# A new order of work and fixed engines in an attention plus two-layer kernel

## The chip, the cores and the metric

One core of one Trainium2 chip. The metric is device microseconds of one execution of the program on that core, the median of several runs. The profiled execution is one more run, taken with the hardware profiler.

## What is computed

Attention with a position bias, then two feed-forward networks, each on 2304 tokens of width 512 with an inner width of 2048:

```python
# _attn_ref: q, k, v are (4, 8, 576, 64)
scores = scale * np.matmul(q, k.transpose(0, 1, 3, 2))
...
x = (psi_rel / psi_i)[..., None]
h = np.maximum(x @ w1 + b1, 0.0)
bias = h @ w2
scores = scores + bias.transpose(2, 0, 1)[None, :, :, :]
scores = scores - np.max(scores, axis=-1, keepdims=True)
attn = np.exp(scores)
attn = attn / (np.sum(attn, axis=-1, keepdims=True) + 1e-09)
return np.matmul(attn, v).astype(np.float32)
...
# _moe_ref
h = x @ w_in
r = np.maximum(h, 0.0)
g = s * (r * r) + b
return (g @ w_out).astype(np.float32)
...
# _moe2_ref
h = x @ w_in
g = h - np.tanh(h)
return (g @ w_out).astype(np.float32)
```

## The kernel before

Matrix products run in f16 on pairs: every operand is split into a high part (a cast) and a low part (what the cast lost), and three products are summed. The splits run on VectorE (`DVE`), ScalarE (`ACT`) and GpSimd (`POOL`); DMAs are issued by SyncE (`SP`).

**Attention** runs over units, each one head of one batch and 128 (or twice 64) query rows: 144 units in groups of four. One unit takes these steps, named by the function inside `unit_tasks` and `unit_rest`: a bias load (`fn`, tile `bi`, DMA), scores (`qk`, two units at a time, L981), bias added and row minimum (`ttr`, L1013 and L1017, VectorE; called the max below, since the sign is turned), exponential (`ex`, L1023, ScalarE), high part (`hi`, L1033 on VectorE or L1035 on ScalarE), low part (`lo`, L1042, GpSimd, two instructions), a DMA transpose of both parts (`tr`, tile `et`, L1048), and the product with the values (`pv`, L1061 and L1067). Every four units `x_tasks` scales the output, splits it and transposes it by DMA into `xt`. The bias itself is made ahead, in 36 strips (`bias_tasks`): hidden values (L667, L670), a matmul (L701), two scaled copies (L558 or L560, tile `et`), a store.

**First feed-forward** (`moe1_tasks`) runs over nine blocks of 256 tokens beside the attention: matmuls into `ph` (L1477), relu and square, high and low part (L1500, L1504), matmuls into `po` (L1546), evacuation `out`, store to `x2d`. Its weights arrive as f64, are turned to f32 on VectorE (L1172 to L1178), and split.

**Second feed-forward** starts when attention has given its memory free (`turn`): its weights are loaded and converted too, then 18 steps `k` (half a block each) run `in_product` (tag `I`, L1942) and `out_product` (tag `J`, L2070), seven products of 24 matmuls each per step, with the products of step k-1 written between those of step k. Between the two lie small sums, tanh and splits; each step has seven high casts (L558 on VectorE or L560 on ScalarE, the two-engine lambda in `split`) and seven low parts (L563, VectorE). `prep_tasks` (tag `X`) prepares a block.

**The order of work** is planned when the program is built. Each step is a `Task` with, for every engine that may run it, a cost in us (for a DMA a pair: how long SyncE is held, how long the transfers are busy). `Schedule.forward` replays the machine with these costs: it takes the engine that can start first, and among its ready tasks the one with the least `prio`; the order found is the order in which the instructions are written to each engine. An engine takes its instructions in that order. `prio` is a due time from the code plus a number from `SHIFT` for that task's key (tag and function name). `COST` multiplies a cost by kind and engine. `HOP` is the time until another engine sees a result, `OVER` what is taken off until the engine is free, `LATE` what its own next step waits. A DMA lands `DMA_START` + its transfer time + `DMA_DONE` after its issue if nothing queues. `ONLY` fixes an engine for a kind. A load's base cost stands in the calls of `load`; a transpose's (1.25, 1.4) in `unit_rest`.

Of the kernel before, what the change touches and what calls it, by code (L numbers as in the profile page):

```python
# [30 lines left out]
AHEAD = 6.0  # L31
COST = {
    "u.ex@act": 1.056, "u.hi@act": 1.132, "bias.lambda@act": 1.102, "f.relu@act": 0.952, "f.square@act": 1.145,
    "x.lambda@act": 1.198, "w.lambda@act": 1.131, "scan.sq@act": 1.17, "bias.out@act": 1.146, "f.out@act": 1.282,
    "w.square@act": 1.07, "k.hi@act": 1.147, "s.lambda@act": 1.093, "q.hi@act": 1.201, "v.hi@act": 1.142,
    "u.ttr@dve": 1.025, "f.hi@dve": 1.09, "x.scale@dve": 0.9, "x.hi@dve": 1.03, "u.hi@dve": 1.07, "s.in_done@dve": 1.78,
    "scan.add@dve": 0.73, "f.lambda@dve": 0.96, "s.out_done@dve": 1.2, "u.lo@pool": 0.947, "f.lo@pool": 0.918,
    "bias.lambda@pool": 0.95, "u.qk@pe": 0.885, "u.pv@pe": 0.97,
}
PORT = {"u.ttr": 0.0, "x.scale": 0.0, "scan.add": 0.0, "k.lambda": 0.4, "v.lambda": 0.4, "q.lambda": 0.4, "s.lambda": 0.4,  # L40
    "X.scales": 0.0, "X.sums": 0.0, "f.scales": 0.0, "f.out": 0.0, "f.norm": 0.0, "w.scales": 0.0, "L.scales": 0.0, "scan.lambda": 0.0,
}
ONLY = {"I.fn": "dve", "I.sub": "dve", "J.fn": "dve", "J.c22": "dve", "I.add": "dve", "X.xsum": "dve", "P.wsum": "dve", "u.lo": "pool", "f.lo": "pool"}
EPS, WINDOW, IDLE, BUSY = 0.02, 3.4, 0.6, 0.9
SHIFT = {
# [162 lines left out]
class Schedule:  # L208
# [11 lines left out]
    def add(self, opts, fn, deps=(), prio=0.0, takes=(), uses=(), after=(), share=None):  # L220

        t = Task()
# [2008 lines left out]
```

## Time and profile before

| what | value |
|---|---|
| median of 3 runs | 1087.64 us (1086.15 to 1091.06) |
| profiled execution | 1087.81 us |
| its span, first to last instruction | 1086.0 us |
| mean granted clock of TensorE | 0.945 |
| TensorE matmul busy | 974.0 us, 90% |
| VectorE busy | 888.1 us, 82% |
| ScalarE busy | 685.5 us, 63% |
| GpSimd busy | 345.7 us, 32% |

Engines: PE is the matmul and PEld the weight load of TensorE, DVE VectorE, ACT ScalarE, POOL GpSimd, SP SyncE. A share over the whole span mixes stages with different limits; the rows below are cut by stage. A wait is put down to what ended it last.

### The profile page before, as it was taken

Reading aid. Unit: us, or ns where it says so; the run is one execution under the profiler, and the core shown is the slowest. Engines: PE = TensorE matmul, PEld = TensorE weight load, DVE = VectorE, ACT = ScalarE, POOL = GpSimd, SP = SyncE. Lnnn points to the kernel's source line nnn. Section 1 sums busy time; section 2 is a strip of 40 time slices with the busy share of each in tenths; the row PEclk is TensorE's granted clock in tenths of the full one; section 3 lists DMA queues with packets and bytes.
Section 4 is the critical chain, followed back from the end, with each engine's and each line's share of the span. In section 5 each row is a group of like instructions: output and inputs, shape, how many; then the busy total and the mean of one; then the engine's idle time right before and its main releaser. Section 6 shows DMA issues by size and latency. Waiting matters only on the chain.

```text
span 1086.0 us, 32355 instructions
## 1 busy us (share of the span) xinstructions
PE 974.0 (90%) x13370; PEld 823.4 (76%) x13370; DVE 888.1 (82%) x1881; ACT 685.5 (63%) x1313; POOL 345.7 (32%) x370
## 2 busy tenths in 40 slices
PE   5566788999999899989889898997999999999998
PEld 2222356678877677777678687887999999999998
DVE  6999999758579766876662989898999999998785
ACT  6698888779765666765663475556665546455452
POOL 5024557446473465665752323210000000000000
PEclk9756599999999999999999899998999999999999
DMA  9979987999989999999985903410010110100000
GB/s 340 355 223 232 284 214 143 215 211 264 247 163 202 189 179 188 205 166 175 161 165 115 353 16 114 159 35 6 27 46 32 31 31 22 41 22 22 21 22 21
DMA packets 261443, 153.65 MB, mean 141 GB/s; under 512 B 197680, under 2 KB 229552, under 8 KB 261296
## 3 DMA queue, kind: packets, MB, share of 16 engines
q1 hardware_dynamic: 261296, 151.59, 57.6%
q8 instruction: 104, 1.70, 0.7%
q14 instruction: 43, 0.35, 0.1%
HBM read 84.03 MB, written 20.33 MB: 96 GB/s over the span
## 4 chain that ended last, share of the span: by engine, by line
PE 52%; DVE 16%; DMA 14%; ACT 7%; issue 5%; POOL 4%; SPq 2%; DVEq 0%; ACTq 0%; POOLq 0%
PE acc L2070 13%; PE po L1546 10%; DMA et<-hl 10%; PE pa L1942 9%; PE pb L1942 6%; PE ph L1477 6%; POOL hl L1042 2%; DVE sp L1013 2%; PE po L2070 2%; PE sp L981 2%; POOL hr L1504 2%; PE xp L1061 2%; DVE w1big L1175 1%; ACT e L1023 1%; DVE hr L1500 1%
## 5 line engine op out<-in xcount | busy, mean ns | idle before, releaser
L1042 POOL TENSOR_TENSOR hl<-e,hl 128x64 f16<-128x64 f32 (+1 forms) x288 | 232.7, 831 | 233.1 <-ACT hl L1035 114.1
L1546 PE MATMUL po<-hr,w1big 128*128 128x256 f16 x1728 | 208.5, 277 | 12.4 <-POOL hr L1504 4.8
L1546 PEld LDWEIGHTS <-w1big 128*128 128x128 f16 x1728 | 167.7, 100 | 40.4 <-issue 18.9
L1477 PEld LDWEIGHTS <-w1big 128*128 128x128 f16 x1728 | 166.6, 99 | 25.8 <-issue 6.1
L1942 PEld LDWEIGHTS <-w2big 128*128 128x128 f16 x3024 | 175.7, 99 | 2.4 <-issue 2.3
L2070 PEld LDWEIGHTS <-w1big 128*128 128x128 f16 x3024 | 174.2, 98 | 4.1 <-issue 4.1
L1013 DVE CUSTOM_DVE_ANT_0 sp<-sp,bi 128x576 f32<-128x576 f32 x144 | 109.6, 761 | 45.4 <-PE sp L981 34.0
L1023 ACT ACTIVATE e<-sp,mx 128x576 f32<-128x576 f32 x144 | 105.8, 736 | 58.2 <-DVE mx L1017 48.8
L1504 POOL TENSOR_TENSOR hr<-r,hr 128x512 f16<-128x512 f32 x72 | 99.1, 1378 | 126.1 <-DVE hr L1500 118.0
L1477 PE MATMUL ph<-xt_own,w1big 128*128 128x256 f16 x960 | 111.4, 273 | 0.9 <-ACT r L1490 0.9
L1061 PEld LDWEIGHTS <-et 128*128 128x128 f16 (+1 forms) x1440 | 52.3, 103 | 70.5 <-DMA et<-hl 54.1
L1061 PE MATMUL xp<-vp,et 128*128 128x64 f16 (+1 forms) x1440 | 65.4, 198 | 37.5 <-DMA et<-hl 35.6
L981 PE MATMUL sp<-ks,qs 64*128 64x288 f16 (+1 forms) x960 | 82.0, 302 | 9.9 <-ACT e L1023 7.7
L1477 PE MATMUL ph<-w1big 128*128 128x256 f16 x768 | 90.5, 278 | 0.0
L2070 PE MATMUL acc<-hr,w1big 128*128 128x128 f16 x1296 | 81.5, 221 | 4.0 <-DVE hr L563 4.0
L1035 ACT ACTIVATE hl<-e 128x576 f16<-128x576 f32 x95 | 64.7, 682 | 24.6 <-DMA et<-hl 23.3
L2070 PE MATMUL acc<-w2big,w1big 128*128 128x128 f16 x1296 | 79.0, 219 | 0.0
L1500 DVE CAST hr<-r 128x512 f16<-128x512 f32 x72 | 46.3, 644 | 30.7 <-ACT r L1495 28.0
L981 PEld LDWEIGHTS <-qs 64*128 64x128 f16 (+1 forms) x960 | 45.7, 101 | 33.8 <-issue 21.1
L1490 ACT ACTIVATE r<-ph 128x512 f32<-128x512 f32 x72 | 42.5, 592 | 37.6 <-PE ph L1477 30.0
L1942 PE MATMUL pa<-w1big,w2big 128*128 128x128 f16 x960 | 62.8, 224 | 2.2 <-ACT w1big L1961 2.2
L1495 ACT ACTIVATE r<-r,sq 128x512 f32<-128x512 f32 x72 | 51.7, 720 | 1.1
(222 smaller groups left out, 1696.3 us busy)
## 6 DMA issues: line engine op xcount, KB each, us to landing
bi<-btd SPq DMA_DIRECT2D x64, 288.0 KB, 3.8
w1big<-in_wout SPq DMA_DIRECT2D x12, 1024.0 KB, 6.2
btd<-et SPq DMA_DIRECT2D x36, 295.5 KB, 3.2
w1big<-in_win SPq DMA_DIRECT2D x8, 1024.0 KB, 8.0
w2big<-in_win SPq DMA_DIRECT2D x8, 1024.0 KB, 12.6
x2d<-x SPq DMA_DIRECT2D x36, 128.0 KB, 2.3
w1big<-x2d SPq DMA_DIRECT2D x36, 128.0 KB, 2.5
outT<-xt_own SPq DMA_DIRECT2D x18, 256.0 KB, 2.2
```

Source lines behind the costliest of these rows:

```text
L981: nc.tensor.matmul(out=out, lhsT=qs.tile[64 * h:64 * h + 64, sq, p * r:p * r + r], rhs=ks.tile[64 * h:64 * h + 64, sk, half * HS:(half + 1 ...
L1013: nc.vector.tensor_tensor_reduce(out=st, in0=st, in1=bi.tile.rearrange("p (a b) -> p a b", a=2), scale=-1.0 / KAP, scalar=3.0e38, op0=ALU. ...
L1023: nc.scalar.activation(out=put(e, row_tile("e")).rearrange("p (a b) -> p a b", a=2), in_=sp.tile[:, :, 0:HS], func=AF.Exp, scale=-1.0, bia ...
L1035: nc.scalar.activation(out=h[:, 0:S], in_=e.tile, func=AF.Copy)
L1042: (nc.gpsimd if eng == POOL else nc.vector).tensor_tensor(out=hl.tile[:, o:o + m], in0=e.tile[:, c:c + m], in1=hl.tile[:, c:c + m], op=ALU ...
L1061: nc.tensor.matmul(out=xp[r0:r0 + r, o:o + 64], lhsT=et.tile[:, n, r0:r0 + r], rhs=vp.tile[:, 0, n % 5, 64 * h:64 * h + 64], start=n == 0, ...
L1477: nc.tensor.matmul(out=ph.tile[:, fi, :], lhsT=win_ap(1, sw, m, f), rhs=xa(sx, m), start=m == 0 and j == 0, stop=m == KM - 1 and j == 2,)
L1500: nc.vector.tensor_copy(out=rh[:, :, 0, :], in_=r.tile)
L1504: (nc.gpsimd if e == POOL else nc.vector).tensor_tensor(out=rh[:, :, 1, :], in0=r.tile, in1=rh[:, :, 0, :], op=ALU.subtract)
L1546: nc.tensor.matmul(out=po.tile[:, :NB1], lhsT=wout_ap(1, sw, f, c), rhs=rhl[f // 8][:, f % 8, sr, :], start=f == 0 and j == 0, stop=f == K ...
L1942: nc.tensor.matmul(out=bank.tile[:, f * HT:(f + 1) * HT], lhsT=w[:, sw, m, f * 128:(f + 1) * 128], rhs=xs[:, sx, m], start=p in (1, 2, 5) ...
L2070: nc.tensor.matmul(out=bank.tile[:, o + c * HT:o + (c + 1) * HT], lhsT=w[:, sw, f, c * 128:(c + 1) * 128], rhs=g[:, sx, f], start=new and ...
```

## The change

Only numbers and how the planner reads them are changed; no task is added or taken away. `COST` gets new values and more keys. `XFER` gives each kind of DMA a factor on its transfer time and a landing time of its own (before: 0.65 us for all). `ENGINE` fixes the engine of two-engine tasks with these keys. `HOP` is larger for pe, dve and pool. Every number of `SHIFT`, some 600, is another one, so that all orders are new.

```diff
-AHEAD = 6.0
+AHEAD = 5.97
 COST = {
-    "u.ex@act": 1.056, "u.hi@act": 1.132, "bias.lambda@act": 1.102, "f.relu@act": 0.952, "f.square@act": 1.145,
...
-    "u.ttr@dve": 1.025, "f.hi@dve": 1.09, "x.scale@dve": 0.9, "x.hi@dve": 1.03, "u.hi@dve": 1.07, "s.in_done@dve": 1.78,
-    "scan.add@dve": 0.73, "f.lambda@dve": 0.96, "s.out_done@dve": 1.2, "u.lo@pool": 0.947, "f.lo@pool": 0.918,
...
+    "u.ex@act": 0.848, "u.hi@act": 1.0283, "bias.lambda@act": 1.1, "f.relu@act": 0.952, "f.square@act": 1.15,
...
+    "u.ttr@dve": 0.8262, "f.hi@dve": 1.1781, "x.scale@dve": 1.04, "x.hi@dve": 1.03, "u.hi@dve": 0.9737,
+    "s.in_done@dve": 1.78, "scan.add@dve": 0.73, "f.lambda@dve": 0.884, "s.out_done@dve": 1.2, "u.lo@pool":
+    1.03, "f.lo@pool": 0.9595, "bias.lambda@pool": 0.992, "u.qk@pe": 0.885, "u.pv@pe": 0.97, "u.tr@sp": 1.17,
+    "x.lambda@sp": 1.07, "q.fn@sp": 1.36, "J.c@dve": 1.13, "J.fn@dve": 1.12, "L.lambda@dve": 1.07,
...
+XFER = {
+    "bias.fn": (0.927, 0.75), "f.fn": (1.133, 0.55), "k.fn": (1.0815, 0.8), "q.fn": (0.8755, 1.15), "scan.fn":
+    (0.9579, 0.8), "u.fn": (1.236, 1.41), "u.tr": (0.9991, 1.54), "v.fn": (1.0712, 1.3), "w.fn": (1.03, 0.87),
+    "x.fn": (1.236, 0.55), "x.lambda": (0.721, 3.44), "L.fn": (0.9991, 0.9), "J.fn": (0.721, 0.3), "X.fn":
+    (1.854, 0.4), "o.fn": (0.8858, 0.0),
+}
...
+ENGINE = {
+    "k1.hi": "act", "f4.out": "act", "u8.hi": "act", "u7.hi": "dve", "I8.lambda": "dve", "I9.lambda": "dve",
+    "X5.lambda": "dve", "I11.lambda": "dve", "I10.lambda": "dve", "bias1.lambda": "act", "I2.lambda": "act",
+    "I1.lambda": "act", "u1.hi": "act", "s4.lambda": "act", "s1.lambda": "act", "I3.lambda": "dve",
+    "I13.lambda": "dve", "X3.lambda": "act", "X2.lambda": "act", "s7.lambda": "act", "I16.lambda": "dve",
+    "u17.hi": "act", "I14.lambda": "act", "bias0.out": "act",
+}
...
 SHIFT = {
-    ".begin": -932.5, ".fn": 1185, ".lambda": 1257, "I0.add": -102.8, "I0.fn": -1616, "I0.lambda": -1827.5,
...
+    ".begin": -392, ".fn": -295.1, ".lambda": -366.4, "I0.add": 1318.5, "I0.fn": 527.2, "I0.lambda": 8.7,
...
 class Schedule:
-    HOP = dict(pe=0.22, act=0.07, dve=0.07, pool=0.1, turn=0.0)
+    HOP = dict(pe=0.33, act=0.07, dve=0.16, pool=0.41, turn=0.0)
     LATE = dict(act=0.034, dve=0.034, pool=0.034)
     OVER = dict(act=0.1, dve=0.085, pool=0.04)
-    DMA_START, DMA_DONE = 1.2, 0.65
+    DMA_START = 1.2
...
-        only = ONLY.get(kind)
-        t.opts = {
-            e: c if isinstance(c, tuple) else c * COST.get(kind + "@" + e, 1.0) for e, c in opts.items()
-            if len(opts) == 1 or only is None or e in only
-        }
+        only = ENGINE.get(t.key) or ONLY.get(kind)
+        t.opts = {}
+        for e, c in opts.items():
+            if len(opts) == 1 or only is None or e in only:
+                if isinstance(c, tuple):
+                    k, d = XFER.get(kind, (1.03, 0.8))
+                    t.opts[e] = (c[0] * COST.get(kind + "@" + e, 1.0), c[1] * k, d)
+                else:
+                    t.opts[e] = c * COST.get(kind + "@" + e, 1.0)
...
                 bus = max(bus, at + self.DMA_START) + cost[1]
-                t.end = t.done = bus + self.DMA_DONE
+                t.end = t.done = bus + cost[2]
```

## Rows read from the trace of the kernel before

**Rows 1.** Stages: length; busy of PE, PEld, DVE, ACT, POOL; clock; DMA share; GB/s.

```profile
27.00:136.00 109.00, 70.51 (x527) 29.61 (x524) 105.52 (x195) 88.86 (x174) 35.53 (x34) 0.64 0.94 273
...
136.00:360.00 224.00, 206.18 (x2667) 160.15 (x2664) 173.86 (x440) 164.78 (x362) 120.33 (x137) 0.97 0.95 208
...
360.00:590.00 230.00, 209.10 (x2859) 170.88 (x2858) 151.79 (x414) 144.33 (x317) 134.65 (x166) 0.99 0.91 170
...
590.00:760.00 170.00, 150.96 (x1438) 133.71 (x1436) 149.37 (x224) 100.88 (x179) 39.94 (x24) 0.94 0.33 116
...
760.00:1060.00 300.00, 300.00 (x5367) 300.00 (x5365) 275.11 (x547) 160.79 (x242) 0.00 (x0) 1.00 0.09 29
```

**Rows 2.** Groups of TensorE, 136 to 590: busy, mean ns, then idle before and releasers.

```profile
L1061 PE MATMUL xp<-vp,et 128*128 128x64 f16 (+1 forms) x1312 | 56.8, 195 | 27.7 <-DMA et<-hl 26.0 <-DVE xf L1107 1.5
```

**Rows 3.** Timeline of TensorE: start, length, what; in brackets idle before, releaser.

```profile
143.06 0.44 PE L1061 MATMUL xp<-vp,et 128*128 128x64 f16 x9 [1.62 <-DMA et<-hl]
...
569.73 0.47 PE L1061 MATMUL xp<-vp,et 128*64 128x64 f16 x18 [1.99 <-DMA et<-hl]
```

**Rows 4.** Source line L1048, the transposes: duration ns and landing us, least/median/most.

```profile
L1048 SPq DMA_TRANSPOSE et<-hl x144: 1242/1344/4131, 72.2 to 578.7; - x144
...
DMA to landing us min/median/max: 3.2/3.9/8.3
```

**Rows 5.** DMA, 136 to 590: queue's share; issues with KB each, median us to landing.

```profile
q1 hardware_dynamic: 204467, 84.87, 92.0%
...
bi<-btd SPq DMA_DIRECT2D x52, 288.0 KB, 3.7
...
xt_own<-xh SPq DMA_TRANSPOSE x28, 2.7
```

**Rows 6.** Groups of VectorE, ScalarE and GpSimd, 136 to 590, columns as rows 2.

```profile
L1013 DVE CUSTOM_DVE_ANT_0 sp<-sp,bi 128x576 f32<-128x576 f32 x126 | 95.9, 761 | 45.2 <-PE sp L981 34.0 <-DMA bi<-btd 5.3 <-ACT scan L793 4.2
...
L1033 DVE CAST hl<-e 128x576 f16<-128x576 f32 x44 | 29.1, 663 | 9.7 <-ACT e L1023 6.7 <-ACT r L1495 2.4 <-DMA et<-hl 0.3
...
L1017 DVE TENSOR_SCALAR mx<-mx 128x1 f32<-128x1 f32 x126 | 19.4, 154 | 4.3
...
L1013 DVE DVE_READ_ACCUMULATOR2_ANT mx<- 128x1 f32 x126 | 17.7, 141 | 0.0
...
L1023 ACT ACTIVATE e<-sp,mx 128x576 f32<-128x576 f32 x126 | 92.6, 735 | 56.1 <-DVE mx L1017 48.0 <-POOL hl L1042 5.0 <-DVE sum L1105 1.3
...
L1035 ACT ACTIVATE hl<-e 128x576 f16<-128x576 f32 x83 | 56.6, 683 | 22.5 <-DMA et<-hl 21.3
...
L1023 ACT ACTIVATION_READ_ACCUMULATOR e<-sp,mx 128x1 f32 x126 | 24.6, 195 | 0.0
...
L1042 POOL TENSOR_TENSOR hl<-e,hl 128x512 f16<-128x512 f32 x255 | 198.9, 803 | 155.6 <-ACT hl L1035 61.2 <-DVE hl L1033 55.3 <-issue 33.0
```

**Rows 7.** Groups of VectorE, 27 to 136: casts that can run on ScalarE too.

```profile
L558 DVE TENSOR_SCALAR et<-pb,cst_sb 128x480 f32<-128x480 f32 (+5 forms) x6 | 2.9, 520 | 0.0
...
L558 DVE TENSOR_SCALAR w1big<-w1big,w_c 128x1024 f16<-128x1024 f32 x2 | 1.5, 745 | 0.0
...
L558 DVE TENSOR_SCALAR ks<-w1big,qkc 128x576 f16<-128x576 f32 x2 | 0.9, 516 | 0.0
```

**Rows 8.** Source line L1033: duration ns least/median/most, first and last start.

```profile
L1033 DVE CAST hl<-e x49: 445/460/1418, 83.7 to 572.7; 128x576 f16<-128x576 f32 x49
```

**Rows 9.** Groups of TensorE, 590 to 760.

```profile
L1546 PE MATMUL po<-hr,w1big 128*128 128x256 f16 x576 | 70.6, 283 | 11.2 <-POOL hr L1504 4.8 <-ACT x L1565 4.3 <-DVE x L1560 1.9
```

**Rows 10.** Stages, columns as rows 1: around blocks 3 and 8 to 11.

```profile
787.00:806.00 19.00, 19.00 (x343) 19.00 (x340) 18.69 (x44) 10.48 (x15) 0.00 (x0) 1.00 0.17 51
...
873.00:949.00 76.00, 76.00 (x1362) 76.00 (x1360) 69.63 (x142) 39.78 (x60) 0.00 (x0) 1.00 0.10 30
```

**Rows 11.** The same stretch, line L558 on VectorE alone.

```profile
873.00:949.00 76.00, 3.58 (x7) 1.00 0.10 30
```

**Rows 12.** Source line L558, one of its tiles, columns as rows 8.

```profile
L558 DVE TENSOR_SCALAR w2big<-w1big,cols x6: 479/488/882, 842.9 to 1030.9; 128x512 f16<-128x512 f32 x4, 128x1280 f16<-128x1280 f32 x2
```

More of the change, by code (lines that the diff above doesn't have):

```diff
@@ L30 @@
 WI0, WI1, WO0, WO1 = 27.23, 74.31, 71.56, 137.63
-AHEAD = 6.0
+AHEAD = 5.97
 COST = {
-    "u.ex@act": 1.056, "u.hi@act": 1.132, "bias.lambda@act": 1.102, "f.relu@act": 0.952, "f.square@act": 1.145,
-    "x.lambda@act": 1.198, "w.lambda@act": 1.131, "scan.sq@act": 1.17, "bias.out@act": 1.146, "f.out@act": 1.282,
-    "w.square@act": 1.07, "k.hi@act": 1.147, "s.lambda@act": 1.093, "q.hi@act": 1.201, "v.hi@act": 1.142,
-    "u.ttr@dve": 1.025, "f.hi@dve": 1.09, "x.scale@dve": 0.9, "x.hi@dve": 1.03, "u.hi@dve": 1.07, "s.in_done@dve": 1.78,
-    "scan.add@dve": 0.73, "f.lambda@dve": 0.96, "s.out_done@dve": 1.2, "u.lo@pool": 0.947, "f.lo@pool": 0.918,
-    "bias.lambda@pool": 0.95, "u.qk@pe": 0.885, "u.pv@pe": 0.97,
+    "u.ex@act": 0.848, "u.hi@act": 1.0283, "bias.lambda@act": 1.1, "f.relu@act": 0.952, "f.square@act": 1.15,
+    "x.lambda@act": 1.2, "w.lambda@act": 1.13, "scan.sq@act": 1.17, "bias.out@act": 1.15, "f.out@act": 1.28,
+    "w.square@act": 1.07, "k.hi@act": 1.15, "s.lambda@act": 1.09, "q.hi@act": 1.2, "v.hi@act": 1.14,
+    "u.ttr@dve": 0.8262, "f.hi@dve": 1.1781, "x.scale@dve": 1.04, "x.hi@dve": 1.03, "u.hi@dve": 0.9737,
+    "s.in_done@dve": 1.78, "scan.add@dve": 0.73, "f.lambda@dve": 0.884, "s.out_done@dve": 1.2, "u.lo@pool":
+    1.03, "f.lo@pool": 0.9595, "bias.lambda@pool": 0.992, "u.qk@pe": 0.885, "u.pv@pe": 0.97, "u.tr@sp": 1.17,
+    "x.lambda@sp": 1.07, "q.fn@sp": 1.36, "J.c@dve": 1.13, "J.fn@dve": 1.12, "L.lambda@dve": 1.07,
+    "L.square@act": 0.919, "P.wsum@dve": 0.942, "X.scales@dve": 0.83, "X.sums@dve": 1.21, "X.xsum@dve": 1.19,
+    "bias.lambda@dve": 0.952, "bias.out@dve": 0.795, "f.norm@dve": 1.27, "f.out@dve": 1.21, "f.scales@dve":
+    1.22, "k.hi@dve": 1.24, "k.lambda@dve": 0.939, "q.hi@dve": 1.06, "s.lambda@dve": 0.952, "scan.lambda@dve":
+    0.857, "v.hi@dve": 1.34, "v.lambda@dve": 0.968, "w.lambda@dve": 0.965, "f.lo@act": 0.95, "f.lo@dve": 0.95,
+    "f.hi@act": 0.99, "f.hi@pool": 0.99, "u.hi@pool": 0.91, "u.ex@dve": 0.8, "u.ex@pool": 0.8, "u.ttr@act":
+    0.81, "u.ttr@pool": 0.81,
+}
```

204 rows, old and new, of the table SHIFT are left out of this document.

## The prediction

> **What bounds the kernel now.** I read the table of stages first. It shows four regimes [rows 1]. From 27 to 136 us VectorE is busy 105.52 of 109 us while TensorE is granted 0.64 of its full clock (a mix of its two levels, 1.2 and 2.4 GHz) and still has idle time: this stage, which converts the first weights, is set by VectorE. From 136 to 590 us (attention beside the first feed-forward) TensorE is busy 206.18 of 224 and 209.10 of 230 us, so it idles 17.8 + 20.9 = 38.7 us, and the DMA engines are as loaded (0.95 and 0.91). From 590 to 760 us (conversion of the second weights beside the end of the first feed-forward) TensorE idles 170 - 150.96 = 19.0 us and is granted 0.94. From 760 to 1060 us TensorE is busy in all of 300 us: nothing but fewer matmuls shortens that, and the change removes none. So what can be won lies ahead of 760.
>
> Second, the groups of TensorE instructions between 136 and 590: one wait carries the idle time. The first matmul of a unit's attention x value product waits 26.0 us in total for the transpose of that unit's exponentials [rows 2]. These are 27 waits, the first of 1.62 and the last of 1.99 us, 0.96 us on average [rows 3].
>
> Third, the landing times. A transpose takes 3.2 / 3.9 / 8.3 us (least, median, most) from issue to landing [rows 4]. The code before plans 1.2 + 1.4 + 0.65 = 3.25 us for it, the least that ever occurs. A full bias load is planned at 1.2 + 0.93 + 0.65 = 2.78 us, and lands after 3.7 us [rows 5].
>
> **Why those waits are there.** One unit in the trace, without the handover between engines: max 0.761 + 0.141 + 0.154, exponential 0.735 + 0.195, high part on ScalarE 0.683, low part on GpSimd 198.9/127.5 = 1.56 (two instructions), transpose 3.9, together 8.13 us [rows 4, 6]. The plan before has 0.974 + 0.824 + 0.679 + 1.42 + 3.25 = 7.15 us (its base costs times `COST`). It is short by 0.98 us, and the mean wait is 0.96 us. TensorE takes its instructions in the written order, so a product that was written for 7.15 us stands there and waits, and the feed-forward matmuls written behind it wait too.
>
> **The change part by part.** No instruction is added or removed; the order on every queue is written anew, and some choices of engine are fixed.
>
> *(A) Fixed engines ahead of 136 us.* `bias0.out`, `bias1.lambda`, `s1`, `s4` and `k1.hi` go to ScalarE. VectorE did three pairs of bias outputs (2.9 us), two weight casts (1.5 us) and two key casts (0.9 us) of these kinds after 27 us [rows 7]. The rows don't tell the tags, so between 0 and 5.3 us leaves VectorE, which sets this stage; ScalarE is busy 88.86 of 109 us there [rows 1] and has room. I take half, -2.5. The other end is +4: casts that are still free may now be written onto VectorE, and eight such casts at 0.5 us are 4 us.
>
> *(B) Later landings, 136 to 590 us.* The plan of one unit becomes 0.785 + 0.661 + 0.617 + 1.545 + (1.2 + 1.40 + 1.54) = 7.75 us, and its handovers grow from 0.53 to 1.04 us. So a product is written between 7.75 - 7.15 = 0.60 and 0.60 + 0.51 = 1.11 us later against its scores. If each of the 27 waits shrinks by that and other matmuls fill the place, 13.4 or 7.0 us of the 26.0 stay (summed wait by wait; the first and the last of the 27 stand in [rows 3]): a gain of 12.6 to 19.0 us. What can take it back: the DMA engines' own share of this stretch, 92.0% [rows 5], leaves 8% of 454 = 36 us, which covers the gain but not much of a detour. And two costs fall below the trace: the max is freed after 0.785 - 0.085 = 0.70 us where its three instructions hold VectorE 1.06 us, the exponential after 0.56 where it holds ScalarE 0.93 us [rows 6]. The plan before was off by 0.17 and 0.21 us there, the new one by 0.36 and 0.37 us. Over the 126 units of this stretch this is 24 us more of unplanned work on VectorE and 20 us on ScalarE; they idle 454 - 325.7 = 128 and 454 - 309.1 = 145 us [rows 1], so it fits, but not everywhere at the right moment. I take -10, with ends -19 and +6; the +6 is one such new shortfall (0.36 - 0.17 = 0.19 us) that reaches TensorE in each of the 32 groups of four units.
>
> The issue of a transpose is now planned at 1.25 x 1.17 = 1.46 us of the SP queue; the trace has 1.24 to 1.34 [rows 4]. Behind it in that queue stand bias and query loads; with 144 x 0.2 = 29 us of slack spread over 500 us they are written a little later than need be. I put nothing on it: late bias loads cost VectorE 5.3 us in all [rows 6], none of it on TensorE. The small transposes of the output rows go from a planned 2.5 to 5.1 us; the trace has 2.7 [rows 5]. So a feed-forward block may be written 2.4 us later than it could start; matmuls of other units stand ahead of it and cover that, so I count nothing. Without that cover it is 2.4 us for each of the six blocks of this stretch, 14 us, which no other step asks for; the range holds a third of it.
>
> Twenty-four high casts (`u1`, `u8`, `u17`) go to ScalarE at 0.683 us, four (`u7`) to VectorE. A cast on VectorE takes 0.445 / 0.460 / 1.418 us [rows 8]; the long ones lie beside a GpSimd subtraction. *The Trainium skill* (SBUF — State Buffer, Who interferes with whom) says that VectorE in a two-port mode and GpSimd exclude each other for the whole instruction, where the code charges a share of 0.65. The trace's spread from 0.445 to 1.418 agrees with a full block now and then; by the rule the four casts would cost at most 4 x 0.96 = 3.8 us of VectorE, against 4 x 0.20 = 0.8 by the mean of 0.663 [rows 6]. That is hidden in the 128 us either way.
>
> *(C) 590 to 760 us.* Planned landings of the weight loads and of the block stores change by under 0.3 us (a store from 2.21 to 2.16, a load of the second weights from 5.02 to 5.27). The 19.0 us idle sit on feed-forward outputs that wait for GpSimd and for the evacuation (11.2 us) [rows 9]; only a lucky order moves them. Ends -6 and +6, I take -1.
>
> *(D) The last stage.* `I3`, `I8` to `I11`, `I13` and `I16` get all seven casts on VectorE (0.488 us each [rows 12]), `X5` too (0.488 and 0.882). One block lasts 18.8 us here, so blocks 8 to 11 lie at about 881 to 956. In the nearest window VectorE is busy 69.63 of 76 us [rows 10], 3.58 of it casts [rows 11]; with 28 casts and `X5` it becomes 69.63 - 3.58 + 13.7 + 1.4 = 81.1 us: 5.1 too many. Around block 3 it idles 19 - 18.69 = 0.3 us [rows 10] and seven casts are 3.4: up to 3.1 too many. TensorE needs a product's input only a block later, so a backlog of some microseconds is hidden if that cover holds; if it is gone, this costs up to 5.1 + 3.1 = 8.2 us, in the one stage that had no idle time. I take +1.
>
> **Sum.** -2.5 - 10 - 1 + 1 = -12.5 us. The profiled execution took 1087.81 us, of it 1086.0 span; the median of the runs is 1087.64, so the same sum holds for both: **1075 us**.
>
> **Rivals.** *The landing correction works (1069 to 1081, chance 0.42)*: above. For it speaks that 0.98 us missing and 0.96 us of wait are the same size. *It works at its far ends (about 1064, chance 0.17)*: B -19 and A -5.3 with D at 0. For it speaks that DMA still has its 36 us; against it the two costs that fell. *The transfers set the stage (1087, chance 0.24)*: with the DMA engines at 0.92 a transpose lands when the engines get to it, not when it is issued; products written later then hold back the buffers of the next unit, and the wait moves from the product to the scores. Such waits are there already (max for scores, 34.0 us [rows 6]). The gain of B is then 0 to 3 and the rest cancels. That the change does nothing is this case too. *VectorE becomes the bound of the last stage (1094, chance 0.17)*: the place is D, the price up to 8.2 us, and it decides once VectorE's backlog exceeds what lies between a product's cast and its use; with B and C together at -2 that is 1087.6 + 8.2 - 2. Against it: the plan charges a cast there 0.49 us, what the trace has, so this load is seen when the order is written.
>
> **How the numbers follow.** A measurement of this kernel tells about 0.5% from no change, 5.4 us: faster is below 1082.2, slower above 1093.1. Faster 0.42 + 0.17 = 0.59, rounded 0.6; within 0.24, less the edge of the first case, 0.23; slower 0.17. The range leaves about 0.1 out at each end: low where A and B stand at their far ends with C and D against them, 1062; high a little above the last rival, 1095.
>
> **What would show it.** Right: between 136 and 590 the 26.0 us wait for the transpose falls below 15, and the same work ends near 577; `et` still lands after about 3.9 us. Wrong in B: that wait stays above 20, or shrinks while the wait of scores for exponentials or of max for scores grows by as much. Wrong in D: TensorE idle between 760 and 1060, with waits for VectorE. Wrong in A: the start of steady scores doesn't come earlier than 136. What would make the whole wrong is a stage ahead of 136 that runs several microseconds longer, since no row of mine tells its new order.

## Result and the profile after

| what | before | after |
|---|---|---|
| median | 1089.35 us (4 runs, 1086.15 to 1093.49) | 1074.64 us (4 runs, 1072.90 to 1077.55) |
| ratio | | 0.9866, 95% interval 0.9822 to 0.9909 |
| profiled execution, its span | 1087.81, 1086.0 us | 1072.90, 1071.1 us |
| TensorE busy, mean granted clock | 974.0 us, 0.945 | 962.1 us, 0.951 |
| VectorE busy | 888.1 us | 898.9 us |

The changed kernel is 14.7 us faster by the medians; 12.5 us were forecast. The stages of after first, cut at the same times as [rows 1] (line numbers of after are those of before plus 22); columns: length; busy of PE, PEld, DVE, ACT, POOL; clock; DMA share; GB/s.

```profile
27.00:136.00 109.00, 64.34 (x477) 26.43 (x478) 102.05 (x195) 86.28 (x167) 32.96 (x29) 0.69 0.92 266
136.00:360.00 224.00, 203.17 (x2677) 160.45 (x2678) 175.79 (x445) 172.56 (x379) 125.30 (x142) 0.97 0.99 214
360.00:590.00 230.00, 221.24 (x2990) 184.26 (x2988) 159.46 (x427) 147.71 (x319) 138.72 (x170) 0.99 0.93 182
590.00:760.00 170.00, 151.06 (x1601) 134.99 (x1599) 158.37 (x233) 105.75 (x186) 35.74 (x20) 0.97 0.29 100
760.00:1060.00 300.00, 300.00 (x5367) 300.00 (x5365) 282.60 (x578) 135.04 (x201) 0.00 (x0) 1.00 0.09 27
```

TensorE idles 8.8 us between 360 and 590 where it idled 20.9, but 20.8 between 136 and 360 where it idled 17.8. Before 136 it does less (477 matmuls for 527).

Equal times hold unequal work in two orders, so I cut both executions again at the same work: from the start to the max of the 41st unit, from there to the last matmul with the values, to the first matmul of `in_product`, to the last of `out_product`. The count of matmuls in a piece is the test of such a cut: 4374 and 4370 in the second, 1111 in the third, 6162 in the fourth.

Stages of before at these points, columns as above.

```profile
0.00:226.30 226.30, 167.29 (x1739) 93.51 (x1740) 200.88 (x421) 182.52 (x356) 101.72 (x98) 0.80 0.91 248
226.30:582.50 356.20, 326.66 (x4374) 268.08 (x4374) 246.79 (x662) 231.22 (x520) 204.00 (x249) 0.99 0.96 192
582.50:720.90 138.40, 125.57 (x1111) 108.83 (x1104) 115.73 (x176) 78.18 (x150) 39.94 (x24) 0.96 0.40 142
720.90:1081.40 360.50, 354.29 (x6162) 352.98 (x6159) 323.79 (x622) 193.55 (x289) 0.00 (x0) 0.99 0.08 25
```

The same of after.

```profile
0.00:233.60 233.60, 162.86 (x1744) 93.95 (x1745) 202.60 (x416) 184.77 (x362) 106.26 (x99) 0.82 0.90 244
233.60:571.50 337.90, 322.87 (x4370) 268.37 (x4370) 245.75 (x664) 230.52 (x515) 203.76 (x248) 0.99 1.01 200
571.50:705.70 134.20, 122.71 (x1111) 107.25 (x1106) 115.25 (x172) 80.36 (x153) 40.73 (x24) 0.99 0.40 142
705.70:1066.90 361.20, 353.44 (x6162) 350.90 (x6159) 334.35 (x662) 169.03 (x249) 0.00 (x0) 0.99 0.09 27
```

So the whole difference has its places: +7.3, -18.3, -4.2 and +0.7 us, and -0.4 behind the last matmul, together -14.9 (the spans differ by as much). By these cuts the start became slower, and attention beside the first feed-forward from unit 41 on brings more than the whole gain. In that piece TensorE's idle time falls from 29.5 to 15.0 us. These are two single executions. Two runs below, e10 and e11, keep after's order in all that lies ahead of the last stage, and there their first three pieces are each 1.0 to 2.0 us longer than after's: differences of that size in one piece say nothing.

What it waits for is in its groups between 136 and 590, after (columns as [rows 2]).

```profile
L1003 PE MATMUL sp<-ks,qs 64*128 64x288 f16 (+1 forms) x852 | 68.6, 289 | 9.2 <-ACT e L1045 6.7 <-ACT ks L582 1.4 <-DVE ks L585 0.6
L1083 PE MATMUL xp<-vp,et 128*128 128x64 f16 (+1 forms) x1341 | 59.3, 197 | 19.1 <-DMA et<-hl 14.5 <-DVE xf L1129 4.4
```

Against [rows 2] the wait of the products for their transposes is 14.5 us for 26.0. Within the piece from unit 41 to the last product it is 6.5 us where before it was 22.7:

```profile
L1061 PE MATMUL xp<-vp,et 128*128 128x64 f16 (+1 forms) x1098 | 46.5, 195 | 24.4 <-DMA et<-hl 22.7 <-DVE xf L1107 1.5
```

```profile
L1083 PE MATMUL xp<-vp,et 128*128 128x64 f16 (+1 forms) x1098 | 46.6, 195 | 6.6 <-DMA et<-hl 6.5
```

The first of these lines is of before, the second of after, each within its own piece. At the max and the exponential no wait took the place of this one. Two groups of after, 136 to 590, answering to the max and the exponential of [rows 6]: max for scores 26.5 us (34.0 before), exponential for max 35.1 (48.0); the max's wait for the bias (5.3 before) is no longer among its three largest.

```profile
L1035 DVE CUSTOM_DVE_ANT_0 sp<-sp,bi 128x576 f32<-128x576 f32 x126 | 95.9, 761 | 31.9 <-PE sp L1003 26.5 <-ACT x L1587 2.2 <-ACT hl L1057 1.3
L1045 ACT ACTIVATE e<-sp,mx 128x576 f32<-128x576 f32 x128 | 93.9, 734 | 48.4 <-DVE mx L1039 35.1 <-POOL hl L1064 5.5 <-DVE sum L1127 2.4
```

### The profile page after: what moved, and what is told of

Its sections match the earlier page's. It is cut to its first block, busy times and chain, and to the rows that moved or that the text cites. A ratio compares the mean times of both kernels' runs of the same rounds, so it can differ in the third digit from the quotient of the medians.

```text
span 1071.1 us, 32375 instructions
## 1 busy us (share of the span) xinstructions
PE 962.1 (90%) x13370; PEld 820.5 (77%) x13370; DVE 898.9 (84%) x1914; ACT 664.7 (62%) x1279; POOL 350.7 (33%) x371
## 4 chain that ended last, share of the span: by engine, by line
PE 55%; DVE 21%; DMA 12%; ACT 4%; issue 4%; POOL 3%; SPq 1%; DVEq 0%; ACTq 0%; POOLq 0%
PE acc L2092 13%; PE ph L1499 9%; PE pa L1964 8%; PE po L1568 8%; DMA et<-hl 8%; PE pb L1964 6%; PE sp L1003 3%; DVE w1big L585 3%; DVE sp L1035 2%; PE po L2092 2%; PE xp L1083 2%; POOL hr L692 1%; ACT e L1045 1%; DMA w1big<-in_wout 1%; DMA bi<-btd 1%
## 5 line engine op out<-in xcount | busy, mean ns | idle before, releaser
L1568 PE MATMUL po<-hr,w1big 128*128 128x256 f16 x1728 | 205.8, 275 | 13.2 <-ACT x L1587 8.6
L1035 DVE CUSTOM_DVE_ANT_0 sp<-sp,bi 128x576 f32<-128x576 f32 x144 | 109.6, 761 | 31.9 <-PE sp L1003 26.5
L1083 PEld LDWEIGHTS <-et 128*128 128x128 f16 (+1 forms) x1440 | 54.9, 103 | 49.8 <-DMA et<-hl 26.6
L1083 PE MATMUL xp<-vp,et 128*128 128x64 f16 (+1 forms) x1440 | 65.5, 198 | 23.5 <-DMA et<-hl 17.8
L1057 ACT ACTIVATE hl<-e 128x576 f16<-128x576 f32 x100 | 67.5, 680 | 24.4 <-DMA et<-hl 21.1
L1522 DVE CAST hr<-r 128x512 f16<-128x512 f32 x72 | 42.2, 588 | 17.6 <-ACT r L1517 16.0
```

The source lines that it names most:

```text
L1035: nc.vector.tensor_tensor_reduce(out=st, in0=st, in1=bi.tile.rearrange("p (a b) -> p a b", a=2), scale=-1.0 / KAP, scalar=3.0e38, op0=ALU. ...
L1057: nc.scalar.activation(out=h[:, 0:S], in_=e.tile, func=AF.Copy)
L1083: nc.tensor.matmul(out=xp[r0:r0 + r, o:o + 64], lhsT=et.tile[:, n, r0:r0 + r], rhs=vp.tile[:, 0, n % 5, 64 * h:64 * h + 64], start=n == 0, ...
L1568: nc.tensor.matmul(out=po.tile[:, :NB1], lhsT=wout_ap(1, sw, f, c), rhs=rhl[f // 8][:, f % 8, sr, :], start=f == 0 and j == 0, stop=f == K ...
```

## Experiments

Two theories. **T1**, that of the prediction: a product is written about 1 us too early against its unit; writing it later fills TensorE and gives the time. **T2**: in a tight order a product that is written later alone only hands its wait to the steps behind it (the rival "the transfers set the stage" had the same consequence), and the time comes from another order of everything. Each run is compared with before on the same chip; where after is the yardstick, its ratio 0.9866 is.

**Only the products moved.** The order of before (e1, e2) and of after (e3, e4) is kept as planned, and on TensorE's queue each product with the values is put behind every step planned to start less than d us after it, or ahead of those less than d before it, as far as the buffers allow. All work is done.

```diff
     def run(self):
-        self.forward(True)
+        self.order = []
+        self.forward()
+        for t, eng in shift_pv(self.order, 0.9):
+            t.fn(eng)
```

*e1: before, 0.9 us later (128 of 144 products moved).*

> The order of the kernel before on every queue, with one thing changed: 128 of the 144 value products stand later on TensorE, behind the TensorE steps that the plan of before starts within 0.9 us of them (mostly one step). Costs, engines and all other places are those of before. Theory (products were written too early for their transposes): of the 26.0 us that products wait for transposes between 136 and 590 us at most 13 stay, the time falls by 8 to 13 us, to 1075 to 1080. Rival (the gain of the change is that of another order as a whole, the transfers set the stage): the wait moves to scores and exponentials, the time stays within 1083 to 1092.

1087.09 us, ratio 0.9997 (0.9980 to 1.0013). TensorE's groups, 136 to 590:

```profile
L1069 PE MATMUL sp<-ks,qs 64*128 64x288 f16 (+1 forms) x840 | 68.4, 288 | 14.4 <-ACT e L1111 11.2 <-DVE qs L651 2.2 <-DVE ks L651 1.0
L1149 PE MATMUL xp<-vp,et 128*128 128x64 f16 (+1 forms) x1314 | 56.4, 195 | 12.9 <-DMA et<-hl 12.3 <-DVE xf L1195 0.5
```

The 26.0 us became 12.3, between the 13.4 and the 7.0 that the prediction worked out for shifts of 0.60 and 1.11 us. The time didn't move: from unit 41 to the last product it takes 355.5 us, in before 356.2. Scores wait for exponentials 11.2 us instead of 4.5, the scaling of the output on VectorE waits for products 22.6 instead of 14.8, casts wait for a free transposed buffer 27.2 instead of 21.3 (ScalarE) and 9.4 instead of 0.3 (VectorE). This is what T2 says.

*e2: before, 2.0 us later (136 moved).*

> As the run before, with 2.0 us in place of 0.9: 136 of 144 products later, mostly by two steps. Theory: the wait for transposes falls to 3 to 6 us, the time ends at 1072 to 1080; most of what is to be had came with the first 0.9 us. Rival: late products hold the buffers of the next units, so the time rises to 1088 to 1096.

1089.62 us, ratio 1.0011 (0.9989 to 1.0034). The wait for transposes is 2.8 us, scores for exponentials 13.5: the wait can be made nearly to vanish and nothing is won. Of the expectations for both runs the rival's came true.

*e3: after, 1.8 us earlier (126 moved).*

> The order of the changed kernel on every queue, with 126 of 144 value products one or two TensorE steps earlier (past steps that its plan starts within 1.8 us ahead of them). Theory: the wait for transposes, 14.5 us between 130 and 575 us in the changed kernel, comes back to 26 us or more, and the time rises by 8 to 15 us from 1074.6, to 1083 to 1090. Rival: the time stays within 1070 to 1079.

1089.85 us, ratio 1.0004 (0.9983 to 1.0025): the whole gain is gone, as the theory had it.

```profile
L1123 DVE CUSTOM_DVE_ANT_0 sp<-sp,bi 128x576 f32<-128x576 f32 x126 | 96.0, 762 | 51.5 <-PE sp L1091 48.5 <-ACT x L1675 1.7 <-DMA bi<-btd 1.2
L1133 ACT ACTIVATE e<-sp,mx 128x576 f32<-128x576 f32 x128 | 94.0, 735 | 65.7 <-DVE mx L1127 53.5 <-POOL hl L1152 6.3 <-DVE sum L1215 3.4
L1171 PE MATMUL xp<-vp,et 128*128 128x64 f16 (+1 forms) x1339 | 60.5, 198 | 39.0 <-DMA et<-hl 23.2 <-DVE xf L1217 15.6
```

Its groups of the same stretch: products wait 23.2 us for transposes (26 or more were expected) and 15.6 for the scaling, the max 48.5 us for scores. From unit 41 to the last product it takes 350.0 us for after's 337.9. So the place of the products matters in after's order.

*e4: after, 0.9 us later (122 moved).*

> The order of the changed kernel with 122 of 144 value products later by 0.9 us of its plan. Theory: the changed kernel's products stand about right; the wait falls from 14.5 to below 8 us, but this is a few us only: 1069 to 1077. Rival: products that are later still hold up the groups' ends, 1078 to 1086.

1083.85 us, ratio 0.9952 (0.9924 to 0.9979), some 9 us behind after and in the rival's range, although the wait for transposes fell from 14.5 to 6.9 us; scores wait 14.8 us for exponentials, the scaling 35.6 for products. In after's order the products stand about right: 1.8 us earlier costs about 15 us, 0.9 us later about 9.

**Costs and shifts planned anew.** The planner's costs (`COST`, `HOP`, `XFER`) apart from `SHIFT`. Each is a new order of everything, one order of many that the costs allow; e5, e6, e8 and e9 were executed twice each, e7 eight times.

*e5: old costs, `SHIFT` taken as zero. e6: the same with all new costs, no `ENGINE`.*

```diff
-        t.fn, t.prio, t.takes = fn, prio + SHIFT.get(t.key, 0.0), tuple(takes)
+        t.fn, t.prio, t.takes = fn, prio, tuple(takes)
```

> The kernel before planned anew with every number of SHIFT at zero: due times from the code alone, costs of before. Theory 1 (the corrected costs carry the gain, whatever the priorities): this is the base for the next run, somewhere in 1110 to 1180. Theory 2 (the gain sits in priorities and costs that fit each other): also 1110 to 1180, since the old numbers of SHIFT are worth as much to the old costs as the new ones to the new.

> The changed kernel planned anew with SHIFT at zero and no engine fixed: the new costs, landings and handovers alone. Theory 1: 10 to 15 us faster than the run before this one. Theory 2: within 10 us of it, on either side.

e5 1143.01 us, ratio 1.0520 (1.0453 to 1.0588); e6 1100.71, 1.0131 (1.0102 to 1.0161): with `SHIFT` at zero the new costs are worth 42 us, where neither expectation had more than 15. The groups of the products over the whole span, e5 and then e6:

```profile
L1061 PE MATMUL xp<-vp,et 128*128 128x64 f16 (+1 forms) x1440 | 67.0, 200 | 54.2 <-DMA et<-hl 53.5 <-DVE xf L1107 0.4
```

```profile
L1083 PE MATMUL xp<-vp,et 128*128 128x64 f16 (+1 forms) x1440 | 66.3, 199 | 11.9 <-DMA et<-hl 8.3 <-DVE xf L1129 3.1
```

The wait falls by 45.2 us while scores for exponentials stay (28.4 and 28.8). Here the place is filled by other work. Stages of e5 (first two lines) and e6, cut at the last product and the first `in_product`:

```profile
0.00:573.20 573.20, 451.52 (x5709) 326.86 (x5714) 448.60 (x1083) 391.00 (x830) 300.04 (x338) 0.88 0.96 216
573.20:756.40 183.20, 164.87 (x1451) 142.72 (x1446) 120.75 (x192) 89.19 (x170) 52.00 (x31) 0.95 0.31 108
```

```profile
0.00:567.10 567.10, 471.85 (x5913) 344.04 (x5918) 453.58 (x1107) 401.02 (x839) 302.43 (x344) 0.92 0.96 219
567.10:716.20 149.10, 135.54 (x1247) 119.47 (x1242) 110.94 (x172) 81.28 (x157) 40.27 (x25) 1.00 0.37 131
```

Attention ends at much the same time, but e6 has 204 more matmuls done beside it (5913 for 5709), and the piece behind it is 34.1 us shorter. That is what "other matmuls fill the place" takes: feed-forward steps that the planner writes there, not a shift of one step.

*e9: as e5 with `XFER` alone.*

```diff
-                t.end = t.done = bus + self.DMA_DONE
+                t.end = t.done = bus + cost[2]
```

> The kernel before planned anew with SHIFT at zero, with one part of the new costs: the transfer times and landings of XFER. COST, HOP and engines are those of before. Its base is the run with old costs and no SHIFT (1143.0 us, 53.5 us of products waiting for transposes); with all new costs it was 1100.7 and 8.3 us. Theory (the landing is what matters): most of the 42 us come with it, 1098 to 1115, and the wait falls to 8 to 20 us. Rival (the handovers and compute costs matter as much): 1120 to 1143, wait above 30 us.

1119.83 us, ratio 1.0291 (1.0247 to 1.0335). The transfer and landing times bring 23.2 of the 42.3 us, the costs and handovers on the engines the other 19.1; the wait for transposes is 20.8 us. The time lies between the two expectations: both parts matter about alike.

*e7: new costs with before's `SHIFT`, no `ENGINE`. e8: old costs with after's `SHIFT` and `ENGINE`.*

```diff
 SHIFT = {
-    ".begin": -392, ".fn": -295.1, ".lambda": -366.4, "I0.add": 1318.5, "I0.fn": 527.2, "I0.lambda": 8.7,
+    ".begin": -932.5, ".fn": 1185, ".lambda": 1257, "I0.add": -102.8, "I0.fn": -1616, "I0.lambda": -1827.5,
...
```

(the diff of e7; e8 is the other way round on before)

> The new costs, landings and handovers, no engine fixed, with the numbers of SHIFT of before. Theory 1: 1072 to 1084. Theory 2: slower than before, 1095 or more, because the old numbers steer an order that no longer comes about.

> The costs, landings and handovers of before with the new numbers of SHIFT and the new fixed engines. Theory 1: no better than before, 1084 to 1095. Theory 2: 1095 or more, as in the run before this one.

e7 1086.94 us, ratio 0.9990 (0.9965 to 1.0016), which neither expectation had; e8 1134.23, 1.0440 (1.0390 to 1.0489), as theory 2 had it. With e5, e6 and the two kernels this makes a table of medians in us (the kernel before as run beside e5 to e8, the changed kernel as in its result):

| | `SHIFT` zero | `SHIFT` of before | `SHIFT` and `ENGINE` of after |
|---|---|---|---|
| costs of before | 1143.01 | 1088.46 | 1134.23 |
| new costs | 1100.71 | 1086.94 | 1074.64 |

Before's shifts were worth 54.5 us on the old costs and 13.8 on the new ones; after's shifts and fixed engines 26.1 on the new costs and 8.8 on the old (the intervals of e5 and e8 overlap, so this 8.8 may be nothing). So a set of shifts fits one set of costs. On before's shifts the new costs win nothing, although e7 plans every queue anew with the corrected landing times. Its groups between 136 and 590, and its piece from unit 41 to the last product:

```profile
L1005 PE MATMUL sp<-ks,qs 64*128 64x288 f16 (+1 forms) x864 | 70.4, 288 | 11.7 <-ACT e L1047 11.4
L1085 PE MATMUL xp<-vp,et 128*128 128x64 f16 (+1 forms) x1332 | 58.4, 196 | 14.6 <-DMA et<-hl 14.0 <-DVE xf L1131 0.4
```

```profile
230.40:585.10 354.70, 331.08 (x4434) 273.42 (x4436) 249.08 (x672) 231.62 (x513) 205.19 (x248) 0.99 0.97 192
```

Products wait 14.0 us for transposes, as short as in after (14.5), but scores wait 11.4 us for exponentials (4.5 in before, 6.7 in after), and the piece takes 354.7 us, near before's 356.2. (This execution is the slowest of the eight, 5 us above their median.) That before's shifts had already repaired most of the error of the old costs would explain why 42 us show as 15 in the change; it fits the table, but no run shows it apart from other reasons.

**Fixed engines.** After's order is kept and some steps only change their engine.

*e10: all 126 high casts of the last stage on VectorE (68 more). e11: the 49 fixed ones on ScalarE.*

```diff
+    return flip(order, lambda t: t.key[0] == "I" and t.key.endswith(".lambda"), "dve")
```

> The order of the changed kernel on every queue, with the 68 high casts of the last stage that it gives ScalarE moved to VectorE at the same places, so that all 126 are there. Theory (a backlog on VectorE stays hidden only while its load fits): 282.6 + 68 x 0.48 = 315 us of work in 300, so at least 15 us come on top somewhere, 1085 to 1100, with TensorE waiting for VectorE. Rival (the block in between hides even that): within 5 us of 1074.6.

> The order of the changed kernel with the 49 casts of the seven blocks that it fixes on VectorE moved to ScalarE at the same places. VectorE falls to 259 of 300 us, ScalarE rises to 170. Theory (the fixing neither costs nor gains, since TensorE is full either way): 1073 to 1077. Rival (the casts on VectorE were a gain, being 0.48 instead of 0.72 us): 1078 to 1084; or a cost of the step as forecast, 1 us and up: 1068 to 1073.

e10 1096.52 us, ratio 1.0090 (1.0057 to 1.0124), 22 us behind after. Its stage from 760 to 1060, and one of TensorE's groups there, in which the waits are for `cols`, a small VectorE step on the queue that holds the casts:

```profile
760.00:1060.00 300.00, 285.73 (x5047) 284.22 (x5045) 289.79 (x609) 92.77 (x140) 0.00 (x0) 0.99 0.08 26
```

```profile
L745 PE MATMUL psum<-cols,ones 128*128 128x2 f32 x14 | 2.5, 246 | 11.8 <-DVE cols L1907 11.8
```

From the first `in_product` to the last `out_product` it takes 380.7 us instead of 361.2. So VectorE can hold up the last stage, as the theory and the rival of step D had it, at a load that the change doesn't reach. e11: 1077.24 us, ratio 0.9901 (0.9872 to 0.9929), whose interval overlaps after's; TensorE is busy in 300.00 of 300 us, VectorE in 266.20. The time lies at the border of the first two expectations. Where these casts run makes no difference that these runs can tell.

*e12: the fixed early steps (`bias0.out`, `k1.hi`, `s1`, `s4`; 16 of them) on VectorE.*

```diff
+    return flip(order, lambda t: t.key in ("bias0.out", "k1.hi", "s1.lambda", "s4.lambda"), "dve")
```

> The order of the changed kernel with sixteen steps that it fixes on ScalarE (the eight bias outputs of the first strip group, four weight casts, four key casts) moved to VectorE at the same places: about 12 us of VectorE work, most of it ahead of 136 us, where VectorE idles 7 us of 109. Theory (VectorE sets that stage, so fixing them on ScalarE is worth something): the whole run gets 3 to 8 us longer, 1078 to 1083. Rival (something else sets that stage, and the fixing is worth nothing): 1072 to 1077.

1085.74 us, ratio 0.9966 (0.9939 to 0.9993), 11 us behind after, more than the theory's 3 to 8. Its stages to the max of unit 41 and to the last product:

```profile
0.00:242.80 242.80, 167.64 (x1741) 97.58 (x1745) 211.91 (x440) 172.33 (x338) 101.85 (x99) 0.80 0.88 234
242.80:589.10 346.30, 323.48 (x4368) 267.43 (x4368) 244.16 (x664) 230.49 (x515) 203.49 (x248) 0.99 1.01 195
```

VectorE has 9.3 us more to do by unit 41 than in after (211.91 for 202.60), and unit 41 comes 9.2 us later: there VectorE's time is the time, nearly one to one. In the next piece it loses 8.4 us more, though no step of that piece was touched; some 2 us of it can be chance, as e10 and e11 show (the profiled execution is also the slowest of ten, 3 us above their median), and the cause of the rest was not sought.

## Why the prediction was right, and where it was not

The time, 1074.64, lies at the forecast, and sign and place of the gain were right. That it lies so near is in part luck: the largest term, B, rests on a step that failed, and cut at unit 41 A came out 9.8 us above what was taken, B and C together 11.5 below. By its own steps:

**What bounds the kernel: right.** The last stage kept its 300 us of 300, and all that was won lies ahead of it. That VectorE sets the start is shown, for after's order, by e12.

**The shortfall of the plan: right in size.** The wait fell from 26.0 to 14.5 us (13.4 or 7.0 were worked out), transposes land after 3.9 to 4.0 us, nearly as before, and e1, which moves the products by such a shift and changes nothing else, left 12.3.

**"Each wait shrinks and other matmuls fill the place": the step that failed.** It is no step that follows by itself. e1 did the first half to the letter and the time stayed at 0.9997 of before; e2 took the wait away and won nothing. Planning every queue anew with the corrected costs isn't enough either: it filled the place with `SHIFT` at zero (e5 to e6, e9), but on before's shifts (e7) the wait fell to 14.0 us and the time stayed at 0.9990. What wins is the corrected costs together with shifts and engines that belong to them: the new costs bring 59.6 us on after's shifts and engines, and nothing that can be told on before's. The prediction put the gain on the landings and gave `SHIFT`, which the change replaces whole, no term at all.

**B, -10 taken, about -18 measured** by this cut (the piece from unit 41 to the last product, between the far end of -19 and the value taken). The idle time there fell by 14.5 us, 16.2 of it at the wait for transposes; TensorE's busy time for the same matmuls fell by 3.8, whose cause no run tells apart. The gain isn't spread over 136 to 590 as the sum had it: of the 14.5 us that are left, 10.0 lie before 370, where it was 8.5. The +6 of a new shortfall (max and exponential planned too short) didn't come: the waits around both fell, and TensorE's wait of scores for exponentials grew by 2.2 us only (4.5 to 6.7).

**A, -2.5 taken, +7.3 measured up to unit 41, outside its ends.** Work did leave VectorE between 27 and 136 us (105.52 to 102.05), and e12 shows that such work can cost its full length. But by unit 41 VectorE had 1.7 us more to do and 5.6 us more idle time (226.30 - 200.88 = 25.4; 233.60 - 202.60 = 31.0). The first max is 3.8 us earlier (62.4 for 66.2), the 17th level (127.3 for 127.4), the 25th 6.4 us late (176.9 for 170.5), and the first feed-forward starts at 159.7 instead of 151.0. How much of the loss is A's hangs on the cut: the prediction had split A from B at 136 us, and at the 17th max (127 us), where the two orders are level, what is left up to the last product became 10.9 us shorter, near B's -10. From there on, before first, then after:

```profile
127.37:582.50 455.13, 415.26 (x5497) 327.04 (x5494) 332.34 (x861) 313.05 (x685) 259.96 (x306) 0.97 0.94 194
```

```profile
127.28:571.50 444.22, 410.58 (x5505) 329.79 (x5506) 334.79 (x863) 318.18 (x694) 259.04 (x308) 0.97 0.98 200
```

But by then after has done fewer of the conversions of weights from f64 on VectorE (12 of each of the three kinds, before 14, 14 and 13), and its 19th max comes 8.7 us late (146.6 for 137.9): part of the early work was put off, not saved. A and B together are -11.0 by either cut, for -12.5 taken. The step that failed in A is pricing a stage by the steps that change engine, when its whole order is new; the last sentence of the prediction had named this danger. Which choices of the new early order cost the 7 us was not tried. In after's order, having sixteen of the fixed steps on ScalarE instead of VectorE is worth 11 us (e12), twice the 5.3 that I had taken as a bound: I had counted only what VectorE did of these kinds in before, and left out what the frozen order behind loses.

**C, -1 taken, -4.2 measured,** within its ends. Feed-forward outputs wait 9.4 us in this piece where it was 11.2 [rows 9], and TensorE's busy time fell by 2.9 at a granted clock of 0.99 for 0.96:

```profile
L1568 PE MATMUL po<-hr,w1big 128*128 128x256 f16 x504 | 59.2, 277 | 9.4 <-ACT x L1587 6.5 <-POOL hr L1526 2.7
```

**D, +1 taken, +0.7 measured,** too little to tell from nothing. The 5.1 us "too many" came from taking all other VectorE work of the window as the blocks' own. After, around blocks 8 to 11 and then its casts alone:

```profile
862.00:938.00 76.00, 76.00 (x1363) 76.00 (x1361) 73.64 (x145) 26.61 (x40) 0.00 (x0) 1.00 0.10 30
```

```profile
862.00:938.00 76.00, 12.81 (x27) 1.00 0.10 30
```

Without casts VectorE is busy 60.8 us here, and 66.05 in the window of [rows 10, 11], so that window held some 5 us of other VectorE work that doesn't fall on these blocks in after's order. Over the stage VectorE is at 282.60 of 300. That VectorE can become the bound is real (e10, 22 us at 68 more casts); the rival's condition wasn't met, and its price of 8.2 us stays untested.

**The rivals.** "The transfers set the stage" did not hold the time: from unit 41 to the last product about the same bytes went in 18.3 us less, and landings grew by 0.1 (transposes) and 0.3 us (bias loads). But the DMA engines' own queue rose from 94.7% to 100.3%, so by this measure nothing is left there of the 8% that the prediction had counted as room. Whether the transfers set what remains of TensorE's 15.0 us of idle time in that piece was not tried. DMA in this piece, before and then after, columns as [rows 5]:

```profile
q1 hardware_dynamic: 167419, 67.54, 94.7%
...
bi<-btd SPq DMA_DIRECT2D x40, 288.0 KB, 3.8
...
et<-hl SPq DMA_TRANSPOSE x106, 3.9
```

```profile
q1 hardware_dynamic: 166451, 66.75, 100.3%
...
bi<-btd SPq DMA_DIRECT2D x40, 288.0 KB, 4.1
...
et<-hl SPq DMA_TRANSPOSE x105, 4.0
```

The rival's other half, that the wait moves from the products to the scores and the buffers, is what e1 and e2 show for products moved alone.

The low end of the range, 1062, doesn't follow from its words: A and B at their far ends give 1087.6 - 5.3 - 19 = 1063.3, and C and D against them would make it longer.

**Still open:** what the early order loses; what in the new shifts fills the place that e7 leaves empty; how much of the 26 us of after's shifts is search and how much is `ENGINE`; and e5 to e9 are one order each, so their differences of a few microseconds say little, those of 20 to 50 much.

## What to carry to other kernels

A wait at the head of an in-order queue measures how wrong the plan is, not what moving that one step would bring: correct the planner's landing times and handovers, write all queues anew, and look for new shifts, since those found on the old costs don't carry over (here the corrected costs alone gave 1086.94 us with the old shifts and 1100.71 with none). Compare two orders at equal work, with the matmul count as the test of the cut, and judge an engine's load over a whole stage rather than over a window of four blocks. Where an engine sets a stage, price the stage's whole new order, or give its term wide ends.

## What the runs showed of the hardware

The DMA engines' busy share says little on how much later a transfer lands: from unit 41 to the last product it rose from 0.96 to 1.01 and the rate from 192 to 200 GB/s, while a transpose landed after 4.0 instead of 3.9 us (medians) and a full bias load after 4.1 instead of 3.8.

The long casts of [rows 8] have a rule. In before, 17 of the 49 start while GpSimd subtracts, and every one of them ends 0.31 to 0.32 us after that subtraction, so they last 0.56 to 1.42 us; the other 32 take 0.45 to 0.46. One of the 17 (start, length; the first line is two subtractions, back to back):

```profile
188.28 1.43 POOL L1042 TENSOR_TENSOR hl<-e,hl 128x64 f16<-128x64 f32 x2 [0.46 <-POOL hr L1504]
188.90 1.12 DVE L1033 CAST hl<-e 128x576 f16<-128x576 f32 x1 [0.47 <-ACT e L1023]
```

The cast ends at 190.02, the second subtraction at 189.71.
